# Staging buffers, store order, u quarters and store queues in the table stage, and the engine of two adds in the transform, of a two-part kernel

## The chip, the cores and the metric

The kernel runs on one core of a Trainium2 chip. The metric is the device time of one execution in microseconds (us). Before the change, three executions took 2489.95, 2495.92 and 2499.25 us; the median, 2495.92 us, is the time before. The profiled execution has a span of 2497.5 us, and the clock granted to TensorE was 0.968 of full speed on average over it.

Engines are named as the profile names them: PE is TensorE's matmul side and PEld its weight loads, DVE is VectorE, ACT is ScalarE, POOL is GpSimd, SP is SyncE, which here only issues transfers. A `q` behind an engine's name marks the transfers that the engine issues.

## The reference, cut to what matters

Two independent results are computed and laid side by side. Part A is attention with a recurrent memory: 64 segments of 32 rows, each with 8 rows of memory that come out of the segment before it, so that the 64 steps can't be reordered. Part B is a long convolution whose kernel is made from tables of exponentials and angles, done with Fourier transforms.

```python
def _A_ref(x, mem0, Wq, Wk, Wv, Wo, seg_len):          # x: 1 x 2048 x 1024, 32 heads of 128
    mem = mem0
    for s in range(n_seg):
        h = concatenate([mem, x[segment s]])
        q, k, v = h @ Wq, h @ Wk, h @ Wv
        o = softmax(mask(q k^T * scale)) v @ Wo
        mem = o[:, :M, :]; outs.append(o[:, M:, :])

def _B_ref(u, A_re, A_im, B_re, B_im, C_re, C_im, log_dt, Dskip):   # u: 1 x 2048 x 1024, N = 128
    dt = exp(log_dt); logdA = dt * (A_re + 1j * A_im); dB = dt * (B_re + 1j * B_im)
    P = exp(logdA[:, :, None] * l)                     # l = 0 .. 2047
    K = einsum('dn,dnl,dn->dl', C, P, dB).real         # the convolution kernel
    y = irfft(rfft(u, padded) * rfft(K, padded))[:2048]
    return y + u * Dskip

out = concatenate([_A_ref(...), _B_ref(...)], axis=-1)
```

## The kernel before: the parts that the change touches

The program has three stages on the one core. Up to about 500 us it makes part B's tables in 17 frames, and between the table instructions it runs three side jobs: the projections of part A that don't depend on the memory (`P` in the frame's order), the transform of u (`U`) and the turning of the transform's matrices (`M`). Up to about 746 us follows the transform of the convolution kernel with the pointwise products, then the last inverse transforms; from about 815 us on part A's 64 segments run, with the weights that don't fit on the chip loaded again in each segment.

Side job P, slice by slice. A value slice goes from PSUM into a staging tile `vst` and from there to DRAM; a key or query slice goes into one large tile `kst`, whose eight stores are put into a list, `late`, from which every later eviction takes one. `kst` is a single buffer: the next matrix's first eviction can write it only when all eight stores of the matrix before have landed.

```python
slices = [k0 0-7, v0 0-3, q0 0-7, v0 4-7, k1 0-7, v1 0-3, q1 0-7, v1 4-7]      # shortened
for i, (m, t, c) in enumerate(slices):
    for j in range(2):
        a = take([128, 512], F32, "pro")               # PSUM
        ...                                            # 8 or 16 matmuls
        def evict(copy, ...):                          # m == "v"
            if late:
                late.pop(0)()
            vst = vals.tile([128, 2, 2, 128], BF16, name="vst", tag="vst", bufs=3)
            copy(out=vst..., in_=a[:])
            nc.sync.dma_start(out=self.PVd[t]..., in_=vst...)
        def evict(copy, ...):                          # m == "k" or "q"
            if late:
                late.pop(0)()
            if (m, t) not in stage:
                stage[m, t] = self.pool.tile([128, NS, 4, 4, XL], BF16, name="kst", tag="kst")
            copy(out=stage[m, t][:, :, h, g, :], in_=a[:]...)
            # after the 16th: late gets 8 stores PKd<-kst
        if j == 0 and i + 3 < len(slices):
            ws.append(load(i + 3))                     # wsl, 4 buffers, on SyncE's queue
        yield evict
```

Side job U, the transform of u, in quarters `dq` of 256 channels:

```python
def load_uh(dh):                                       # half of the channels, one buffer
    t_ = up.tile([128, 16, DH], BF16, name="u_h", tag="u_h")
    for r in range(4):
        sy.dma_start(out=t_[:, 4 * r:4 * r + 4, :], in_=u_r[r][:, :, DH * dh:DH * dh + DH])
...
for dq in range(4):
    if dq % 2 == 0:
        uv = load_uh(dq // 2)
    for kc in range(4):
        for r in (0, 2, 1, 3):
            ...                                        # 8 matmuls ups<-u_h,MF, evictions, adds on DVE and POOL
```

The kernel values are stored to DRAM (`Kd`) in 30 small pieces for each of four groups; one piece leaves after each exponential, and what is left at the end leaves alternately on SyncE's and GpSimd's queue:

```python
def put(out, in_):
    late.append(lambda eng=gp: eng.dma_start(out=out, in_=in_))
...
for n_, f_ in enumerate(late):                         # at the end of the tables
    f_((sy, gp)[n_ % 2])
```

The pointwise stage: two halves `dh` of the channels, four row blocks `kc`, two `half`. With `dh == 1` two inverse transforms of the other half follow each.

```python
for half in range(2):
    ...                                                # 32 matmuls hps, copy of one result by ACT
    X = pw.tile(...)
    v.tensor_tensor(out=X[:, 0], in0=s_[0][:], in1=o_[:], op=ALU.add)        # L1150
    v.tensor_tensor(out=X[:, 1], in0=s_[0][:], in1=o_[:], op=ALU.subtract)   # L1151
    Y = pw.tile([128, 2, 2, DH], F32, name="y", tag="y", bufs=2)
    for n_, q in enumerate(qs):
        v.tensor_tensor(out=Y[:, n_]..., in0=uc, in1=x_, op=ALU.mult)        # L1157
        v.tensor_tensor(out=x_, in0=un, in1=x_, op=ALU.mult)                 # L1158
    v.tensor_tensor(out=Y[:, :, 0, :], ...)                                  # L1159
    v.tensor_tensor(out=Y[:, :, 1, :], ...)                                  # L1160
    for j, op in ((0, ALU.add), (1, ALU.subtract)):
        (v if (dh, kc, half) == (1, 3, 1) else gp).tensor_tensor(out=Bt[:, kc, half, j], ...)   # L1163
    inverses(2 if dh == 1 else 0)                      # ends with two DVE instructions on uu: L1215, L1216
...
if dh == 0 and kc == 0:
    ks.append(load_k(1, (sy,), ...))                   # 31 loads KT<-Kd for the second half
```

Of the kernel before, what the change touches and what calls it, by code (L numbers as in the profile page):

```python
# [10 lines left out]
BF16 = mybir.dt.bfloat16  # L11
F32 = mybir.dt.float32
# [52 lines left out]
class Ahead:  # L65
# [40 lines left out]
    def projections(self):  # L106

        nc, KC, NS, XL, PKd, xTl = self.nc, self.KC, self.NS, self.XL, self.PKd, self.xTl

        slices = [(m, t, c) for m, t, cs in (("k", 0, (0, 8)), ("v", 0, (0, 4)), ("q", 0, (0, 8)), ("v", 0, (4, 8)), ("k", 1, (0, 8)), ("v", 1, (0, 4)),  # L110
                                             ("q", 1, (0, 8)), ("v", 1, (4, 8))) for c in range(*cs)]

        def load(i):
            m, t, c = slices[i]
            w = self.pool.tile([128, KC, 256], BF16, name="wsl", tag="wsl", bufs=4)
            nc.sync.dma_start(out=w[:], in_=self.src(m)[:, :, 2048 * t + 256 * c:2048 * t + 256 * c + 256].rearrange("k p f -> p k f"))
            return w
        ws = [load(0), load(1), load(2)]
        take, vals = yield
        late = []  # L120

        def rows_out(t):
            for k in range(XL):
                late.append(lambda k=k, t=t: nc.sync.dma_start(out=PKd[:].rearrange("s (h k) f -> k s h f", k=XL)[k][:, :, 512 + 128 * t:640 + 128 * t],
                                  in_=self.PVd[t][:].rearrange("(s k) (h e) -> k s h e", k=XL, e=128)[k]))

        done = {}
        stage = {}
        self.late = late

        def counted(m, t, n, then):
            done[m, t] = done.get((m, t), 0) + 1
            if done[m, t] == n:
                then()

        for i, (m, t, c) in enumerate(slices):
            w = ws[i]
            g, h2 = c // 2, 2 * (c % 2)
            mo = 256 * t + (0 if m == "k" else 128)
            for j in range(2):  # L140
                a = take([128, 512], F32, "pro")
                if m == "v":
                    for b in (2 * j, 2 * j + 1):
                        for kc in range(KC):
                            nc.tensor.matmul(a[:, 256 * (b % 2):256 * (b % 2) + 256], lhsT=xTl[:, kc, 16 * b:16 * b + 16, :].rearrange("p s k -> p (s k)"),
                                             rhs=w[:, kc, :], start=(kc == 0), stop=(kc == KC - 1), skip_group_check=True)

                    def evict(copy, a=a, t=t, c=c, j=j):
                        if late:
                            late.pop(0)()  # L150
                        vst = vals.tile([128, 2, 2, 128], BF16, name="vst", tag="vst", bufs=3)
                        copy(out=vst[:].rearrange("p b h e -> p (b h e)"), in_=a[:])
                        nc.sync.dma_start(out=self.PVd[t][:].rearrange("(b p) f -> p b f", p=128)[:, 2 * j:2 * j + 2, 256 * c:256 * c + 256],
                                          in_=vst[:].rearrange("p b h e -> p b (h e)"))
                        counted("v", t, 16, lambda: rows_out(t))
                else:
                    for kc in range(KC):
                        nc.tensor.matmul(a[:], lhsT=w[:, kc, 128 * j:128 * j + 128], rhs=xTl[:, kc, :, :].rearrange("p s k -> p (s k)"),  # L158
                                         start=(kc == 0), stop=(kc == KC - 1))

                    def evict(copy, a=a, m=m, t=t, g=g, h=h2 + j, mo=mo):
                        if late:
                            late.pop(0)()
                        if (m, t) not in stage:
                            stage[m, t] = self.pool.tile([128, NS, 4, 4, XL], BF16, name="kst", tag="kst")
                        st = stage[m, t]
                        copy(out=st[:, :, h, g, :], in_=a[:].rearrange("p (s k) -> p s k", k=XL))

                        def out():
                            for r in range(8):  # L170
                                late.append(lambda r=r: nc.sync.dma_start(out=PKd[8 * r:8 * r + 8, :, mo:mo + 128].rearrange("s p f -> p s f"),
                                                                          in_=st[:, 8 * r:8 * r + 8].rearrange("p s a b c -> p s (a b c)")))
                        counted(m, t, 16, out)
                if j == 0 and i + 3 < len(slices):
                    ws.append(load(i + 3))
                yield evict
# [420 lines left out]
def part_b(ctx, tc, u, A_re, A_im, B_re, B_im, C_re, C_im, log_dt, Dskip, out_b, ahead, copies, residents):  # L597
# [5 lines left out]
    DH, DQ = 512, 256  # L603
# [207 lines left out]

    u_r = u.rearrange("(c p r) d -> r p c d", p=128, r=4)

    def load_uh(dh):
        t_ = up.tile([128, 16, DH], BF16, name="u_h", tag="u_h")
        for r in range(4):
            sy.dma_start(out=t_[:, 4 * r:4 * r + 4, :], in_=u_r[r][:, :, DH * dh:DH * dh + DH])
        return t_[:].rearrange("p c (t s e) -> p c s t e", t=4, e=8)


    def take(shape, dtype, name):
        return ps_k.tile(shape, dtype, name=name, tag="s")
# [13 lines left out]

    def side():

        for dq in range(4):
            if dq % 2 == 0:  # L840
                uv = load_uh(dq // 2)
            for kc in range(4):
                got = {}
                for r in (0, 2, 1, 3):
                    ps = take([128, 2, DQ], F32, "ups")
                    for cs in range(2):
                        for mc in range(4):
                            pe.matmul(ps[:, cs, :], lhsT=MF[:, 4 * r + mc, cs, 128 * kc:128 * kc + 128], rhs=uv[:, 4 * r + mc, 8 * (dq % 2):8 * (dq % 2) + 8],
                                      start=(mc == 0), stop=(mc == 3), skip_group_check=True)

                    def evict(copy, r=r, ps=ps, got=got, dq=dq, kc=kc):
                        if r == 0:
                            got["a"] = up.tile([128, 2, 2, DQ], F32, name="ua", tag="ua")
                        a_ = got["a"]
                        if r < 2:
                            copy(out=a_[:, r], in_=ps[:])
                            return
                        s_ = got[r] = up.tile([128, 2, 2, DQ], F32, name="us", tag="us", bufs=3)
                        v.tensor_tensor(out=s_[:, 0], in0=a_[:, r - 2], in1=ps[:], op=ALU.add)
                        v.tensor_tensor(out=s_[:, 1], in0=a_[:, r - 2], in1=ps[:], op=ALU.subtract)  # L860
                        if r == 3:
                            e_, o_ = got[2], s_
                            x_ = up.tile([128, 4, 2, DQ], F32, name="ux", tag="ux")
                            gp.tensor_tensor(out=x_[:, 0], in0=e_[:, 0], in1=o_[:, 0], op=ALU.add)
                            gp.tensor_tensor(out=x_[:, 2], in0=e_[:, 0], in1=o_[:, 0], op=ALU.subtract)
                            for q, cs, op in ((1, 0, ALU.subtract), (1, 1, ALU.add), (3, 0, ALU.add), (3, 1, ALU.subtract)):
                                gp.tensor_tensor(out=x_[:, q, cs], in0=e_[:, 1, cs], in1=o_[:, 1, 1 - cs], op=op)
                            gp.dma_start(out=Ud[kc, dq], in_=x_[:])
                    yield evict
# [34 lines left out]
    late = []  # L904

    def put(out, in_):
        late.append(lambda eng=gp: eng.dma_start(out=out, in_=in_))

    def put_values(sb):
        kx = KxT["t"]  # L910
# [215 lines left out]
    def pointwise(dh, kc, KT, Bt):  # L1126
        us = spectra.pop(0)
        for half in range(2):
# [20 lines left out]
            X = pw.tile([128, 2, 2, DH], F32, name="x", tag="x")  # L1149
            v.tensor_tensor(out=X[:, 0], in0=s_[0][:], in1=o_[:], op=ALU.add)  # L1150
            v.tensor_tensor(out=X[:, 1], in0=s_[0][:], in1=o_[:], op=ALU.subtract)  # L1151
            Y = pw.tile([128, 2, 2, DH], F32, name="y", tag="y", bufs=2)
            split = "p c (a d) -> p c a d"
            for n_, q in enumerate(qs):
                uc, un = (us[q][:, :, i, :].unsqueeze(1).to_broadcast([128, 2, 2, DQ]) for i in range(2))
# [4 lines left out]
            v.tensor_tensor(out=Y[:, :, 1, :], in0=Y[:, :, 1, :], in1=X[:, :, 0, :], op=ALU.add)  # L1160
            first = 0 if half == 0 else 1
            for j, op in ((0, ALU.add), (1, ALU.subtract)):
                (v if (dh, kc, half) == (1, 3, 1) else gp).tensor_tensor(out=Bt[:, kc, half, j], in0=Y[:, first], in1=Y[:, 1 - first], op=op)  # L1163
            inverses(2 if dh == 1 else 0)

    NIV = 3
# [55 lines left out]
    for dh in range(2):  # L1222
# [8 lines left out]
        for kc in range(4):  # L1231
            pointwise(dh, kc, ks[dh], Bt)
            if kc < 3 or dh == 0:
                spectra.append(load_u(dh + (kc + 1) // 4, (kc + 1) % 4))
            if dh == 0 and kc == 0:
                ks.append(load_k(1, (sy,), ktp.tile([128, 16, DH], BF16, name="KT", tag="KT")))
    ctx2.close()
    ctx_m.close()
    for c in range(16):
# [97 lines left out]
```

## Time and profile before

| Of the profile's page | value |
|---|---|
| span | 2497.5 us |
| PE busy | 2021.1 us, 81% |
| DVE busy | 1480.5 us, 59% |
| ACT busy | 965.7 us, 39% |
| POOL busy | 411.4 us, 16% |
| vst, 128x512, evicted by DVE | 20 times, mean 681 ns |
| vst, 128x512, evicted by ACT | 12 times, mean 582 ns |
| kst, 128x512, evicted by DVE / ACT | 43 times, mean 685 ns / 21 times, mean 581 ns |
| Bt on POOL, 128x1024 | 30 times, mean 2556 ns |
| Bt on DVE, 128x1024 | 2 times, mean 1222 ns |
| Kd stores issued by POOL / SP | 102 / 18 |

How to read it: busy times are sums over the span, and the three stages have different limits. A group's row gives the engine, the tile written and the tile read, the count and the mean of one. The row of an engine's waits names who released it last. A time line gives for each instruction its start, its length and, in brackets, how long the engine sat idle before it and who ended that.

### The profile page before, as it was taken

The page shows a single profiled execution, that of the slowest core. Times are in us where ns is not written, and L with a number is a line of the kernel's source. Part 1 is how long each engine was busy: PE and PEld are TensorE (multiplying, and loading weights), DVE is VectorE, ACT ScalarE, POOL GpSimd, SP SyncE. Part 2 cuts the span into 40 slices and gives each one's busy share as a digit, 9 for nine tenths or more (in the row PEclk, how much of TensorE's full clock was granted, in tenths as well). Part 3 has the DMA queues.
Part 4 walks back from the last instruction along what each step waited for, and adds up shares of the span by engine and source line. Part 5 has one row for each costly group of instructions (what it writes and reads, how often), then busy time and mean ns, then how long its engine had stood idle before and what let it go on. Part 6 is the DMA issues. An engine that isn't in the chain of part 4 may idle for free.

```text
span 2497.5 us, 76340 instructions
## 1 busy us (share of the span) xinstructions
PE 2021.1 (81%) x32774; PEld 1080.4 (43%) x32774; DVE 1480.5 (59%) x3129; ACT 965.7 (39%) x1543; POOL 411.4 (16%) x628
## 2 busy tenths in 40 slices
PE   1689888785968688888888888887888888888879
PEld 1356564532423244444444444444444444444444
DVE  9589888979791354545454545454545454545540
ACT  6679788811212132333333323232323233333321
POOL 2235565634331100000000000000000000000010
PEclk9999999888989799999999999999999999999999
DMA  6675965654339999999999999999999999999992
GB/s 161 191 217 167 272 167 149 167 162 144 107 132 347 346 378 378 374 390 365 380 378 373 363 369 387 370 367 359 383 377 371 385 378 380 379 384 374 389 368 90
DMA packets 384778, 763.17 MB, mean 306 GB/s; under 512 B 119462, under 2 KB 213638, under 8 KB 382390
## 3 DMA queue, kind: packets, MB, share of 16 engines
q1 hardware_dynamic: 365638, 702.56, 78.3%
q0 software_dynamic: 13888, 37.89, 4.6%
q10 hardware_dynamic: 4912, 17.84, 2.0%
q8 instruction: 256, 4.19, 0.7%
q14 instruction: 84, 0.69, 0.1%
HBM read 703.35 MB, written 67.88 MB: 309 GB/s over the span
## 4 chain that ended last, share of the span: by engine, by line
DMA 31%; PE 23%; DVE 8%; ACT 3%; issue 2%; SPq 1%; ACTq 0%; DVEq 0%
DMA wst<-WD_k 15%; PE acc L339 13%; DMA wst<-WD_o 11%; PE pp L438 3%; DMA wst<-WD_v 3%; PE pe L561 2%; PE tr L350 2%; DMA wst<-WD_q 1%; DVE piece L278 1%; ACT ev L345 1%; DMA W_o<-in_A_Wo_dram 1%; PE pv L411 1%; DVE ob L527 1%; ACT ob L528 1%; DVE sc L378 1%
## 5 line engine op out<-in xcount | busy, mean ns | idle before, releaser
L339 PEld LDWEIGHTS <-hT 128*32 128x32 bf16 x12352 | 326.0, 97 | 467.4 <-issue 245.4
L339 PE MATMUL acc<-wst,hT 128*32 128x512 bf16 x3072 | 312.6, 391 | 158.9 <-DMA wst<-WD_k 66.2
L345 ACT CAST ev<-acc 128x512 bf16<-128x512 f32 x384 | 225.1, 586 | 406.5 <-PE acc L339 401.6
L438 PEld LDWEIGHTS <-oT 128*32 128x32 bf16 x8192 | 203.1, 96 | 124.4 <-issue 97.8
L278 DVE TENSOR_SCALAR piece<-keep 128x256 int32<-128x256 int32 (+1 forms) x640 | 191.2, 363 | 52.4 <-PE pp L438 32.5
L438 PE MATMUL pp<-W_o,oT 128*32 128x256 bf16 x5120 | 210.6, 275 | 7.5 <-DMA W_o<-in_A_Wo_dram 7.5
L339 PE MATMUL acc<-W_v,hT 128*32 128x512 bf16 x3072 | 210.9, 379 | 0.0
L377 DVE TENSOR_REDUCE mx<-sc 128x8 f32<-128x320 f32 x128 | 62.4, 488 | 247.0 <-PE sc L370 246.7
L339 PE MATMUL acc<-W,hT 128*32 128x512 bf16 x2560 | 206.2, 393 | 0.0
L351 DVE COPY KT<-tr 128x512 bf16<-128x512 bf16 x64 | 27.2, 425 | 260.5 <-PE tr L350 260.5
L358 POOL COPY KT<-pk 128x128 bf16<-128x128 bf16 x128 | 37.7, 295 | 809.2 <-PE sc L370 444.5
L438 PE MATMUL pp<-wst,oT 128*32 128x256 bf16 x2560 | 128.7, 277 | 45.4 <-DMA wst<-WD_o 36.1
L351 ACT COPY QT<-tr 128x512 bf16<-128x512 bf16 x128 | 75.0, 586 | 190.5 <-PE tr L350 189.6
L1209 PE MATMUL yp<-Bt,mi 128*128 128x512 bf16 x384 | 112.3, 400 | 44.2 <-DMA mi<-MId 32.4
L312 POOL COPY hT<-xt 128x192 bf16<-128x192 bf16 x64 | 22.2, 348 | 729.3 <-DMA xt<-XTd 574.4
L425 ACT CAST oT<-pv 128x512 bf16<-128x512 f32 x128 | 75.0, 586 | 166.4 <-PE pv L411 165.0
L339 PE MATMUL acc<-W_q,hT 128*32 128x512 bf16 x1792 | 134.7, 382 | 0.0
L158 PE MATMUL pro<-xTl,wsl 128*128 128x512 bf16 x512 | 121.7, 389 | 5.2 <-ACT xTl L102 5.2
L379 ACT ACTIVATE sc<-sc 128x320 f32<-128x320 f32 x128 | 54.0, 422 | 154.2 <-DVE sc L378 148.8
L339 PE MATMUL acc<-W_k,hT 128*32 128x512 bf16 x1536 | 108.7, 390 | 0.0
L1137 PE MATMUL hps<-KT,MF 128*128 128x512 bf16 x384 | 96.4, 402 | 15.0 <-DVE x L1151 14.4
L350 PE MATMUL tr<-a_ident,ev 128*128 128x128 bf16 x1024 | 101.8, 222 | 1.0 <-ACT KT L351 1.0
(280 smaller groups left out, 3700.4 us busy)
## 6 DMA issues: line engine op xcount, KB each, us to landing
wst<-WD_o SPq DMA_DIRECT2D x320, 512.0 KB
wst<-WD_k SPq DMA_DIRECT2D x256, 512.0 KB
wst<-WD_q SPq DMA_DIRECT2D x256, 512.0 KB
wst<-WD_v SPq DMA_DIRECT2D x256, 512.0 KB
Ud<-ux POOLq DMA_DIRECT2D x16, 1024.0 KB, 5.7
uq<-Ud SPq DMA_DIRECT2D x32, 512.0 KB
pk<-PKd SPq DMA_DIRECT2D x64, 192.0 KB
wsl<-in_A_Wk_dram SPq DMA_DIRECT2D x16, 512.0 KB
```

Of the source, the lines that this page charges most:

```text
L158: nc.tensor.matmul(a[:], lhsT=w[:, kc, 128 * j:128 * j + 128], rhs=xTl[:, kc, :, :].rearrange("p s k -> p (s k)"), start=(kc == 0), stop=( ...
L278: nc.vector.tensor_scalar(out=out.bitcast(I32), in0=in_.bitcast(I32), scalar1=0, scalar2=None, op0=ALU.bitwise_or)
L339: nc.tensor.matmul(a[32 * g:32 * g + 32, o_:o_ + rhs.shape[1]], lhsT=hT[:, kc, :], rhs=rhs, start=(kc == 0), stop=(kc == KC - 1), tile_pos ...
L345: nc.scalar.copy(out=q[:], in_=a[:])
L350: nc.tensor.transpose(out=p[:, i, hl, :, :].rearrange("p a b -> p (a b)"), in_=q[:, 128 * hl:128 * hl + 128], identity=ident[:])
L351: eng(out=dst, in_=p[:, i, :, :, :])
L377: nc.vector.tensor_reduce(out=mx[:], in_=sc, axis=AX.X, op=ALU.max)
L379: nc.scalar.activation(out=sc, in_=sc, func=ACT.Exp, scale=scale)
L425: nc.scalar.copy(out=o[:], in_=p[:].rearrange("p a (g q) -> p a g q", g=4))
L438: nc.tensor.matmul(po[32 * qt:32 * qt + 32, :], lhsT=oT[:, h % 4, (h % 16) // 4, :], rhs=columns(w, 1024 * hh + 256 * qt, 256)[0][1], star ...
L1137: pe.matmul(ps[:, cs, :], lhsT=MF[:, 4 * rr + mc, cs, 128 * kc:128 * kc + 128], rhs=rhs, start=(i == 0 and mc == 0), stop=(i == 1 and mc = ...
L1209: pe.matmul(yp[:], lhsT=m_[:, cs, kc, :], rhs=Bt[:, kc, half, j, c_, :], start=(n == 0), stop=(n == 15))
```

## The change

It touches two stages. In the table stage it gives the value staging tile six buffers, takes up to two stores from the list at every eviction, loads u by quarters of the channels into two tiles (so that the next quarter can be loaded while one is used), and puts the kernel-value stores on SyncE's queue. In the transform it puts the two last pointwise instructions on VectorE throughout, with one buffer for Y, and moves the second half's kernel loads to GpSimd's queue. The aim of the first part is to take away waits for buffers in the tables. The diff, with unchanged lines cut:

```diff
                     def evict(copy, a=a, t=t, c=c, j=j):
-                        if late:
+                        for _ in range(min(2, len(late))):
                             late.pop(0)()
-                        vst = vals.tile([128, 2, 2, 128], BF16, name="vst", tag="vst", bufs=3)
+                        vst = vals.tile([128, 2, 2, 128], BF16, name="vst", tag="vst", bufs=6)
...
                     def evict(copy, a=a, m=m, t=t, g=g, h=h2 + j, mo=mo):
-                        if late:
+                        for _ in range(min(2, len(late))):
                             late.pop(0)()
...
-    def load_uh(dh):
-        t_ = up.tile([128, 16, DH], BF16, name="u_h", tag="u_h")
-        for r in range(4):
-            sy.dma_start(out=t_[:, 4 * r:4 * r + 4, :], in_=u_r[r][:, :, DH * dh:DH * dh + DH])
+    u_q = u.rearrange("(c p r) (d t q s) -> r d q p c t s", p=128, r=4, d=2, t=4, q=2)
+    def load_uq(dq):
+        t_ = up.tile([128, 16, 4, 64], BF16, name="u_h", tag="u_h%d" % (dq % 2))
+        for c in range(16):
+            sy.dma_start(out=t_[:, c], in_=u_q[c // 4][dq // 2][dq % 2][:, c % 4])
...
+        uvs = [load_uq(0), load_uq(1)]
         for dq in range(4):
-            if dq % 2 == 0:
-                uv = load_uh(dq // 2)
+            uv = uvs.pop(0)
+            if dq in (1, 2):
+                uvs.append(load_uq(dq + 1))
...
-        late.append(lambda eng=gp: eng.dma_start(out=out, in_=in_))
+        late.append(lambda eng=sy: eng.dma_start(out=out, in_=in_))
...
-            Y = pw.tile([128, 2, 2, DH], F32, name="y", tag="y", bufs=2)
+            Y = pw.tile([128, 2, 2, DH], F32, name="y", tag="y")
...
-                (v if (dh, kc, half) == (1, 3, 1) else gp).tensor_tensor(out=Bt[:, kc, half, j], in0=Y[:, first], in1=Y[:, 1 - first], op=op)
+                v.tensor_tensor(out=Bt[:, kc, half, j], in0=Y[:, first], in1=Y[:, 1 - first], op=op)
...
-                ks.append(load_k(1, (sy,), ktp.tile([128, 16, DH], BF16, name="KT", tag="KT")))
+                ks.append(load_k(1, (gp,), ktp.tile([128, 16, DH], BF16, name="KT", tag="KT")))
```

More of the change, by code (lines that the diff above doesn't have):

```diff
@@ L812, in part_b @@
     u_r = u.rearrange("(c p r) d -> r p c d", p=128, r=4)
-    def load_uh(dh):
-        t_ = up.tile([128, 16, DH], BF16, name="u_h", tag="u_h")
-        for r in range(4):
-            sy.dma_start(out=t_[:, 4 * r:4 * r + 4, :], in_=u_r[r][:, :, DH * dh:DH * dh + DH])
-        return t_[:].rearrange("p c (t s e) -> p c s t e", t=4, e=8)
+    u_q = u.rearrange("(c p r) (d t q s) -> r d q p c t s", p=128, r=4, d=2, t=4, q=2)
[3 more added lines that the diff above has]
+            sy.dma_start(out=t_[:, c], in_=u_q[c // 4][dq // 2][dq % 2][:, c % 4])
+        return t_[:].rearrange("p c t (s e) -> p c s t e", e=8)
     def take(shape, dtype, name):
@@ L847, in side @@
                         for mc in range(4):
-                            pe.matmul(ps[:, cs, :], lhsT=MF[:, 4 * r + mc, cs, 128 * kc:128 * kc + 128], rhs=uv[:, 4 * r + mc, 8 * (dq % 2):8 * (dq % 2) + 8],
+                            pe.matmul(ps[:, cs, :], lhsT=MF[:, 4 * r + mc, cs, 128 * kc:128 * kc + 128], rhs=uv[:, 4 * r + mc],
                                       start=(mc == 0), stop=(mc == 3), skip_group_check=True)
```

## The prediction, made before the changed kernel ran

> **What bounds the kernel now.** I read the chain of waits first, to see which stage a change can move, then the time lines of the two stages that the change touches, and the table of waits of the table stage.
>
> ```profile
> ## 4 chain that ended last, share of the span: by engine, by line
> DMA 31%; PE 23%; DVE 8%; ACT 3%; issue 2%; SPq 1%; ACTq 0%; DVEq 0%
> ```
>
> The chain, followed backwards, reaches only to 819.88 us, where part A's segments start. From there it is weight transfers (DMA 31%) and matmuls, which the change leaves alone. So part A keeps its length, and the change counts by how far it moves the end of the pointwise stage (746 us): after that the DMA engines are 88 to 104% busy with weights that need the memory freed there, so I carry a shift of that point over one to one.
>
> The table stage, read from ScalarE's time line. Each frame loads the exponential table once, so the distance of two such loads is a frame:
>
> ```profile
> 201.97 1.28 ACT L1003 ACT_TABLE_LOAD   x1
> 224.99 1.28 ACT L1003 ACT_TABLE_LOAD   x1
> 248.00 1.28 ACT L1003 ACT_TABLE_LOAD   x1
> 273.49 1.28 ACT L1003 ACT_TABLE_LOAD   x1
> 303.66 1.28 ACT L1003 ACT_TABLE_LOAD   x1
> ```
>
> Two frames take 23.02 us, the next ones 25.49 and 30.17. In the 23 us frames ACT is busy 94% and DVE 95%, which is their floor. The waits of 70 to 520 us say what the longer frames wait for:
>
> ```profile
> ACT vst L152 <- DMA PVd<-vst: 12.2, 4, 4.5
> DVE kst L167 <- DMA PVd<-vst: 8.7, 2, 4.6
> ACT kst L167 <- DMA PVd<-vst: 4.5, 2, 2.6
> ACT kst L167 <- DMA PKd<-kst: 2.2, 1, 2.2
> PEld L848 <- DMA u_h<-in_B_u_dram: 1.0, 1, 1.0
> ```
>
> (Total us, times, longest.) The first row is the three staging tiles used up. The next three are one thing: the first eviction of a new matrix waits for the single kst buffer; that two rows name PVd I take as the view's choice of the transfer that came last. The u load is nearly free of waits.
>
> The pointwise stage, from the time lines of DVE and POOL:
>
> ```profile
> 526.27 4.66 POOL L1163 TENSOR_TENSOR Bt<-y 128x1024 bf16<-128x1024 f32 x2 [8.72 <-DMA Dsk<-in_B_Dskip_dram]
> 529.13 1.23 DVE L1150 TENSOR_TENSOR x<-hps,osb__7233 128x1024 f32<-128x1024 f32 x1 [3.09 <-ACT osb__7233 L1145]
> ...
> 538.77 1.23 DVE L1150 TENSOR_TENSOR x<-hps,osb__7322 128x1024 f32<-128x1024 f32 x1
> ...
> 542.29 3.25 DVE L1158 TENSOR_TENSOR x<-uq,x 128x1024 f32<-128x1024 f32 x1
> ...
> 638.35 0.42 DVE L1215 TENSOR_TENSOR uu<-uu,Dsk 128x512 bf16<-128x512 bf16 x1
> 638.52 4.95 POOL L1163 TENSOR_TENSOR Bt<-y 128x1024 bf16<-128x1024 f32 x2 [10.55 <-DVE y L1160]
> 638.88 2.38 DVE L1216 TENSOR_TENSOR uu<-uu,yb 128x512 bf16<-128x512 bf16 x1
> 641.18 2.57 DVE L1215 TENSOR_TENSOR uu<-uu,Dsk 128x512 bf16<-128x512 bf16 x1
> 643.86 0.43 DVE L1216 TENSOR_TENSOR uu<-uu,yb 128x512 bf16<-128x512 bf16 x1
> ```
>
> The reader is to see that DVE runs without gaps here (it is the bound of this stage), and that an instruction that takes 0.42 or 1.23 us takes about 2 us more while POOL's Bt instruction runs.
>
> **What the Trainium skill says.** "SBUF — State Buffer", section "Who interferes with whom": a VectorE instruction with two SBUF inputs contends with a GpSimd instruction that reads SBUF; who comes first holds the shared ports for the whole instruction. The lines above agree: 2.38 against 0.43 us. The same section infers that writing descriptors for a transfer issued by GpSimd does not disturb two-input instructions; no line here shows it, and I need it for the 31 kernel loads that move to POOL. "DMA: Bandwidth & Descriptors", section "Why small descriptors are slow (HBM only)", gives a fixed cost per packet. The trace's DMA records agree: packets of 256 bytes on SyncE's queue took 18 ns, of 512 bytes 27, of 1024 bytes 46. "TensorE: Matmul & The Clock Gate", section "What's actually happening", says that idleness throttles TensorE. The trace agrees: where the kst wait is (280 to 290 us) the clock fell to 0.66.
>
> **The change part by part.**
>
> Tables. The distances from 123.44 us on are 23.03, 26.68, 28.82, 23.02, 23.01, 25.49, 30.17, 23.03, 23.01, 26.78, 29.58, 23.01, 23.02, 23.51. Over 23.02 they add to 3.66 + 2.47 + 3.76 + 0.49 = 10.4 us in the frames of the vst wait and 5.80 + 7.15 + 6.56 = 19.5 us in those of the kst wait. The latter hold about 4 us of wait and after it matmuls at half clock. Six vst buffers cover the six value evictions of one frame (144.0 to about 161 us; the seventh comes at 171 us), so the 10.4 go. With two stores per eviction the eight kst stores leave in four evictions, about 156 instead of 172 us, and the next matrix starts at about 177 us; stores land within 10 us, so the 19.5 go too. Of 29.9 us I take 27, with 3 for new waits on SyncE's queue.
>
> That queue gets 84 kernel-value stores and 64 u loads in place of 8. In the built program every transfer on it waits for the one eight places ahead. At 0.5 to 0.8 us each, as in this trace (18 such stores took 14.03 us), a frame's some 25 transfers need about 17 of 23 us: full, but not the bound. The u quarters are runs of 128 bytes. From 32-byte packets at 15 ns and 256-byte ones at 18 I estimate 16 ns: 8192 packets x 16 ns / 16 engines = 8.2 us per quarter. The first two quarters, 32 issues x 0.55 us = 17.6 us, push the next weight slice from 95.87 to about 111 us; PE needs it at about 120 us. No gain and no loss; the u wait removed is about 1 us.
>
> The seam of the stages. The built program has nine more kernel-value stores on SyncE's queue between the 31 first kernel loads and the last stores; 9 x 0.6 = 5 us. The last stores, which before were issued up to 522.7 us and released POOL's first Bt at 526.27, come 5 us later against the rest. That wait moves to DVE, because Bt lies where the kernel values did: DVE would reach its first Bt at 516.5 + 8 x 1.2 = 526.2, and waits until about 531. Loss 5 us.
>
> Pointwise, first half. A period now: (597.54 - 538.77) / 5 = 11.75 us, of which 9.64 (529.13 to 538.77) is undisturbed work. New: 9.64 + 2 x 1.15 for Bt = 11.95. The first two periods were undisturbed already and so get 2.3 us longer; of the first, 1.6 fits into a gap of 3.09. Sum to the start of the last period: +3.3 us. The second half begins with the mi loads, which wait for DVE's last reading of uq, and that comes 2.3 us earlier in a period without POOL: together +1.0, with the seam +6.
>
> Pointwise, second half. There POOL delays two uu instructions by 2 us each, 4.1 us per period. In place of it come 2.3 us of Bt plus some 0.1. So 15.30 becomes 13.9 (PE needs 64 matmuls x 0.217 = 13.9, which is the new floor), 21.03 becomes 19.4, and 19.24 becomes 17.6. Three of the first and three of the others: 3 x 1.4 + 3 x 1.6 = 9 us. I take 7, since waits for uq (5.64, 3.87 and 3.85 us) and mi hang on transfers and can give some back.
>
> Sum: -27 + 5 + 1 - 7 = -28 us. 2495.9 - 28 = 2468 us.
>
> **The rivals.** First: SyncE's queue becomes the bound of the tables. For it: in-order issue, eight in flight, 140 transfers more, and stretches with the DMA engines over 100% busy (150 to 160 us). Then value and weight transfers come late, frames stay at 25 to 30 us, and the change is worth 0 to -10 us. Against it: the queue stood idle for some 15 us in every frame without value slices. Second: moving Bt to DVE costs its full price, 30 x 1.22 = 37 us, with the contention of now hidden in waits anyway; then transform +15 to +20 and the sum is about -5. Against it: DVE has no gaps in the first half, so the delays by POOL are real time. Third: the seam costs nothing and the second half gives its 9 us; sum -36. Fourth: part A's start is set by DMA work that goes on anyway, so that a part of the gain is lost there; little speaks for it, since those loads wait for the memory of the stage before.
>
> **Range and chances.** The before itself spreads over 9 us. The table gain is safe to perhaps 8 us, seam and transform to about 6 each: 2452 to 2484 us holds it 8 times in 10. 2% is 50 us, more than all the parts together can give (29.9 + 9), so faster by over 2% gets 0.05; slower by over 2% would need the first two rivals and more, 0.02; within 2% 0.93.
>
> **What would show each step.** Frames all near 23.0 us between the table loads, no wait of vst or kst for a store, and PE's clock near 1.0 from 280 to 290 and 380 to 390 us: the table step. The end of the tables (last KxT eviction, 506.1 us) near 479 us. A DVE wait of about 5 us before its first Bt: the seam. Bt on DVE 32 times at 1.22 us, L1158 and L1216 never above 1.3 and 0.5 us, periods of 12 us in the first half and 14 to 19 in the second: the transform. Wrong I would be by frames above 24 us whose waits name wsl, u_h or Kd, by PE waits in the pointwise stage beyond those for mi, or by a first segment of part A that does not move with 746 us.

## The result and the profile after

The changed kernel takes 2458.59 us (median of 4 executions, 2452.7 to 2462.8) against 2497.59 us before: a ratio of 0.9843, 95% interval 0.9805 to 0.9881. Predicted were 2468 us, with a range of 2452 to 2484 us, and a gain below 2%; the gain is 39.0 us where 28 were predicted. The table lays the two profiles side by side at the points at which the prediction's steps end.

| point in the trace | before, us | after, us | moved | prediction |
|---|---|---|---|---|
| last KxT eviction (end of the tables) | 506.11 | 476.83 | -29.3 | -27 |
| second X (past the seam) | 529.13 | 499.59 | -29.5 | -22 |
| second X of the second half | 628.90 | 599.51 | -29.4 | -21 |
| last Bt (end of the pointwise stage) | 746.23 | 706.44 | -39.8 | -28 |
| weight load wst<-WD_k at the start of part A's segments | 819.88 | 781.65 | -38.2 | -28 |
| end of the span | 2497.5 | 2459.8 | -37.7 | -28 |

The chain of waits on the page of the changed kernel:

```profile
## 4 chain that ended last, share of the span: by engine, by line
DMA 33%; PE 30%; DVE 15%; issue 13%; ACT 6%; SPq 1%; POOL 1%; DVEq 0%; ACTq 0%; POOLq 0%
```

Its shares add up to 99% where those of before added up to 68%: it is followed back to the start of the span now. But between 516 and 753 us most of it is "issue", time in which the view names no wait; the longest piece, 79.6 us from 515.94 us on, is the time before GpSimd's first store of a result. So the chain doesn't show what bounds the pointwise stage, and VectorE's time line is used for that below. DMA and PE still carry most of the chain. The last three rows of the table show that the shift of the pointwise stage's end reaches the end of the program almost whole.

The frames, from ScalarE's time line of the changed kernel (start, length, engine, line; line numbers are 3 higher than before):

```profile
238.96 1.28 ACT L1006 ACT_TABLE_LOAD   x1
261.98 1.28 ACT L1006 ACT_TABLE_LOAD   x1
285.00 1.28 ACT L1006 ACT_TABLE_LOAD   x1
```

All distances are 23.0 us; only one of the fourteen behind the first frame is longer than 23.04 (23.41 us). The excess over the floor fell from 29.9 to 0.4 us. The waits of 70 to 520 us, cut to the rows in which a write to a staging tile waits:

```profile
DVE kst L167 <- PE pro L158: 17.4, 4, 7.6
...
ACT kst L167 <- PE pro L158: 7.7, 3, 3.7
```

What is left are waits for matmuls (PE pro), that is for the tile's input; these stood in the kernel before too (20.3 and 7.2 us). All rows that name a store are gone. TensorE's granted clock from 280 to 290 us, 0.66 before, is 1.00.

The pointwise stage, from VectorE's time line of the changed kernel:

```profile
496.60 2.36 DVE L1166 TENSOR_TENSOR Bt<-y 128x1024 bf16<-128x1024 f32 x2
...
620.15 1.23 DVE L1160 TENSOR_TENSOR y<-uq,x 128x1024 f32<-128x1024 f32 x1 [4.54 <-DMA uq<-Ud]
```

The first Bt has no bracket: VectorE doesn't wait for it, and the seam costs nothing. The groups of instructions by shape give the trade on VectorE, first of the kernel before, then of the changed one (busy us, mean ns of one | idle before):

```profile
L1158 DVE TENSOR_TENSOR x<-uq,x 128x1024 f32<-128x1024 f32 x32 | 47.3, 1478 | 1.1
...
L1215 DVE TENSOR_TENSOR uu<-uu,Dsk 128x512 bf16<-128x512 bf16 x32 | 28.5, 891 | 13.8 <-DMA uu<-in_B_u_dram 13.6
```

```profile
L1161 DVE TENSOR_TENSOR x<-uq,x 128x1024 f32<-128x1024 f32 x32 | 39.2, 1225 | 1.1
...
L1166 DVE TENSOR_TENSOR Bt<-y 128x1024 bf16<-128x1024 f32 x32 | 37.8, 1222 | 0.5
...
L1218 DVE TENSOR_TENSOR uu<-uu,Dsk 128x512 bf16<-128x512 bf16 x32 | 13.5, 420 | 13.0 <-DMA uu<-in_B_u_dram 13.0
```

L1158 (now L1161) falls by 8.1 and L1215 (now L1218) by 15.0 us. Of the groups not shown, L1157 falls from 45.5 to 39.0 and L1216 from 27.3 to 13.6 us; that is 43.3 us in all. Bt adds 37.8 us less the 2.4 of its two instructions of before, 35.4 us. VectorE ends with 8 us less work than before in these groups, although it got 30 instructions more. The waits for uq (one of them is the last line of the time line above) stay as they were, 13.4 us before and 13.1 after.

How far a total can be trusted: in one set, 54 executions of the kernel before lay between 2477.96 and 2511.51 us. In the profiles of this study the part behind the pointwise stage, which is the same program throughout, took 1737 to 1753 us. Below, stage ends therefore carry the reasons (those of the changed kernel agreed within 2 us in two profiles: 706.44 and 708.21), and totals are given with their intervals.

### The profile page after: what moved, and what is told of

Same layout as the page of the kernel before. It is cut to its first block, busy times and chain, and to the rows that moved or that the text cites. A ratio compares the mean times of both kernels' runs of the same rounds, so it can differ in the third digit from the quotient of the medians.

```text
span 2459.8 us, 76393 instructions
## 1 busy us (share of the span) xinstructions
PE 2017.1 (82%) x32774; PEld 1082.4 (44%) x32774; DVE 1470.8 (60%) x3159; ACT 963.6 (39%) x1543; POOL 303.5 (12%) x545
## 4 chain that ended last, share of the span: by engine, by line
DMA 33%; PE 30%; DVE 15%; issue 13%; ACT 6%; SPq 1%; POOL 1%; DVEq 0%; ACTq 0%; POOLq 0%
DMA wst<-WD_k 15%; PE acc L339 13%; DMA wst<-WD_o 10%; PE pp L438 3%; DMA wst<-WD_q 3%; PE pe L561 2%; PE pro L158 2%; DMA wst<-WD_v 2%; DVE nr L1029 2%; PE tr L350 2%; PE ups L851 2%; PE pa L998 1%; DVE piece L278 1%; ACT ev L345 1%; ACT E L1006 1%
## 5 line engine op out<-in xcount | busy, mean ns | idle before, releaser
L438 PE MATMUL pp<-wst,oT 128*32 128x256 bf16 x2560 | 129.0, 278 | 39.4 <-DMA wst<-WD_o 30.1
```

Source lines behind the costliest of these rows:

```text
L438: nc.tensor.matmul(po[32 * qt:32 * qt + 32, :], lhsT=oT[:, h % 4, (h % 16) // 4, :], rhs=columns(w, 1024 * hh + 256 * qt, 256)[0][1], star ...
```

## The experiments

### The table edits alone (e1_tables)

On the kernel before, in both evictions and at the value tile:

```diff
-                        if late:
+                        for _ in range(min(2, len(late))):
...
-                        vst = vals.tile([128, 2, 2, 128], BF16, name="vst", tag="vst", bufs=3)
+                        vst = vals.tile([128, 2, 2, 128], BF16, name="vst", tag="vst", bufs=6)
```

> The kernel before with only the two edits of the table evictions: six staging tiles for values and two stores per eviction. Kernel value stores stay on GpSimd, u stays in halves, Bt stays on GpSimd. Theory (the 29.5 us of the tables come from the two staging waits alone): all frames from 123 us on take 23.0 us, the last KxT eviction comes near 477 us instead of 506, the pointwise stage keeps its length, and the time is about 29 us less, 2468. Rival (the other queue and the u quarters had a part in it): some frames stay at 24 to 28 us, and 5 to 15 us of the gain are missing, 2475 to 2485.

Measured: 2484.31 us, ratio 0.9962 (0.9943 to 0.9982). The last KxT eviction comes at 494.49 us, 11.6 earlier and not 29. All frames take 23.0 us (one 23.37) but one, which ScalarE's time line shows between these two loads:

```profile
286.11 1.28 ACT L1003 ACT_TABLE_LOAD   x1
326.15 1.28 ACT L1003 ACT_TABLE_LOAD   x1
```

40.04 us in place of 23.0, and TensorE's time line says why:

```profile
298.98 1.89 PE L848 MATMUL ups<-u_h,MF 128*128 128x256 bf16 x8 [16.59 <-DMA u_h<-in_B_u_dram]
```

TensorE stands 16.59 us for the second half of u, for which the profile of before showed a wait of 1.0 us. So the rival holds, and by more than it said: the staging edits without the u quarters give less than half of the tables' gain.

### Each of the two edits alone (e5_vst and e6_two)

```diff
-                        vst = vals.tile([128, 2, 2, 128], BF16, name="vst", tag="vst", bufs=3)
+                        vst = vals.tile([128, 2, 2, 128], BF16, name="vst", tag="vst", bufs=6)
```

> The kernel before with six value staging tiles as the only edit. Theory (two separate waits, the rows that name the value stores for the kernel staging tile are the view's choice): the ScalarE wait of vst is gone, and the frames that begin with a new projection matrix keep 5 to 7 us over 23.0; excess of the frames about 20 us in place of 29.9, plus whatever of the u wait shows once the frames before it are faster. Rival (one cause: value stores hold up the kernel staging tile too): excess under 5 us apart from a u wait.

```diff
-                        if late:
+                        for _ in range(min(2, len(late))):
```

> The kernel before with two stores per eviction as the only edit. Theory: the kst waits are gone, the vst waits stay or grow; excess of the frames about 10 us in place of 29.9, plus whatever of the u wait shows. Rival (the staging tile of the kernels is free only after value stores land, so that earlier issue does not help): excess 25 us or more.

Measured with six tiles alone: excess 19.6 us, as the theory said, nearly all of it in three frames of 29.57, 29.86 and 28.73 us (both kernels of this section ran once, so only their frames and waits are read); two of the waits (total, times, longest) that are left:

```profile
DVE kst L167 <- DMA PVd<-vst: 10.3, 2, 5.3
...
PE ups L848 <- DMA u_h<-in_B_u_dram: 1.6, 1, 1.6
```

Value tiles are plentiful here, and the row of the kernel tile still names PVd: reading them as the view's choice of the last transfer was right. With two stores alone:

```profile
PE ups L848 <- DMA u_h<-in_B_u_dram: 15.4, 1, 15.4
ACT vst L152 <- DMA PVd<-vst: 15.1, 4, 5.4
```

No kst row that names a store is left, but the excess is 32.7 us, more than before, and the last KxT eviction comes at 509.67 us. That is a total in the range of the rival, but without its cause: the kst waits are gone, as the theory said. The vst waits grew from 12.2 to 15.1 us, and the u wait came out. Taken with e1, this orders the three waits: the u wait is 1.6 us where the kst waits stand, and 15 to 17 us in both kernels where they are gone. They hide it.

### The u halves in the changed kernel (e8_uh)

```diff
-    def load_uq(dq):
-        t_ = up.tile([128, 16, 4, 64], BF16, name="u_h", tag="u_h%d" % (dq % 2))
-        for c in range(16):
-            sy.dma_start(out=t_[:, c], in_=u_q[c // 4][dq // 2][dq % 2][:, c % 4])
+    def load_uh(dh):
+        t_ = up.tile([128, 16, DH], BF16, name="u_h", tag="u_h")
+        for r in range(4):
+            sy.dma_start(out=t_[:, 4 * r:4 * r + 4, :], in_=u_r[r][:, :, DH * dh:DH * dh + DH])
```

> The changed kernel with u in two halves of four issues again, one tile. Theory (the 17 us wait for u seen when only the table edits were made comes from the single u tile, filled only after its last reader, behind other transfers on SyncE's queue): one frame at 277 to 310 us takes about 40 us, all others 23.0; last KxT eviction near 494 instead of 477 us; about 2474. Rival (the wait came from kernel value stores on GpSimd, and is gone with them on SyncE): no such frame, 2459.

Measured: 2475.5 us, ratio 0.9918 (0.99 to 0.9937). One frame takes 40.14 us, all others 23.02 to 23.05, and the last KxT eviction comes at 494.33 us: in the changed kernel the u quarters are worth 17.5 us. The kernel value stores are on SyncE here; e1, with them on GpSimd, has the same wait, so the rival, GpSimd's stores as the cause, is out. SyncE's own time line of this kernel, and TensorE's next line, show the wait's parts:

```profile
288.18 0.58 SPq L116 DMA_DIRECT2D wsl<-in_A_Wk_dram  x1
288.87 6.47 SPq L817 DMA_DIRECT2D u_h<-in_B_u_dram  x4
```

```profile
297.86 1.89 PE L848 MATMUL ups<-u_h,MF 128*128 128x256 bf16 x8 [15.91 <-DMA u_h<-in_B_u_dram]
```

TensorE has been idle since 297.86 - 15.91 = 281.95 us, so from then on the tile has no reader and could be loaded. The load is issued only at 288.87, because the queue works through other transfers first (PKd, Kd, WD_o and, as the first line shows, a weight slice): 6.9 us. The other 9.0 us pass from the issue of the load to its landing. The clock follows: from 280 to 300 us it is 0.65 here and 1.00 in the changed kernel. This agrees with the Trainium skill, "TensorE: Matmul & The Clock Gate", section "What's actually happening", that idleness throttles TensorE.

### The queue edits alone (e3_queues)

On the kernel before: the u quarters as in the change, and

```diff
-        late.append(lambda eng=gp: eng.dma_start(out=out, in_=in_))
+        late.append(lambda eng=sy: eng.dma_start(out=out, in_=in_))
```

> The kernel before with only the two queue edits: kernel value stores of the frames on SyncE instead of GpSimd, u loaded by quarters with 64 issues. Theory (neither is on the path; they only make room): frames with value slices keep their excess of about 30 us in all, time 2495 to 2500. Rival (SyncE's queue becomes a bound while the staging tiles are still few, since each value store now stands behind kernel value stores): frames get longer, 2505 to 2515.

Measured: 2494.14 us, ratio 1.0012 (0.9984 to 1.0039); excess of the frames 31.0 us, last KxT eviction 508.23. The theory holds: without the staging edits these two edits gain nothing that can be measured, and SyncE's queue does not become a bound. So the parts don't add: staging edits alone 11.6 us, the two queue edits alone nothing, all together 29 us.

### Kernel value stores back on GpSimd (e7_kd_gp)

On the changed kernel, the edit of e3's diff the other way round.

> The changed kernel with the kernel value stores of the frames on GpSimd's queue again; u quarters, six value tiles and two stores per eviction stay. Theory (the move of these stores to SyncE has no part in the gain, and GpSimd's descriptor writing does not slow VectorE): all frames 23.0 us, last KxT eviction within 2 us of 477, pointwise as in the changed kernel, 2459. Rival (GpSimd falls behind, and VectorE waits for the KxT tile): frames of 24 us and more, 2465 to 2475.

Measured: 2457.04 us, ratio 0.9852 (0.9825 to 0.988); the changed kernel in the same set 0.9858 (0.9833 to 0.9883). In the total no part of the move can be seen. In the profile the last KxT eviction comes at 482.87 us, 5.9 later than in the changed kernel's profile of that set (477.01), which neither theory said: the first table load came 1.2 later, the first frame was 1.5 longer, and one frame took 26.29 us, in which TensorE waited 3.0 us for a weight slice.

The wait for a weight slice also stood in one frame of the next experiment (27.67 us), where these stores are on SyncE, cost 0.4 us in the first profile of the changed kernel and no frame is lengthened in its second. It can't be put down to the moved stores; where the other 2.7 us come from stays open. What the wait hangs on is seen on SyncE's time line of the changed kernel:

```profile
288.39 14.22 SPq L819 DMA_DIRECT2D u_h<-in_B_u_dram  x16
302.72 0.45 SPq L116 DMA_DIRECT2D wsl<-in_A_Wk_dram  x1
```

The 16 issues of the last u quarter stand directly ahead of the slice. In the four profiles (changed kernel twice, this one, the next) the slice is issued at 302.72, 301.51, 305.81 and 305.06 us, and TensorE's wait for it ends 4.3 to 4.5 us later in each; the wait is 1.8, 1.2, 3.0 and 4.4 us. So it depends on when the slice is issued. How late that is differs from run to run: the 16 issues took 13.0 to 18.2 us, and in the next experiment the queue was 3.6 us behind when it came to them.

### All left-over stores on SyncE (e4_seam)

```diff
-        f_((sy, gp)[n_ % 2])
+        f_(sy)
```

> The changed kernel with all 36 stores left over at the end of the tables on SyncE instead of half of them on GpSimd. Theory (in the changed kernel the stores land shortly before VectorE needs the memory, so that a delay within the slack is free and beyond it costs one to one): issues at 0.77 us end near 507 instead of 493 us, VectorE waits 10 to 13 us before its first Bt, and the uq loads behind them can add some; 2470 to 2478. Rival (the seam has large slack and never shows): no such wait, 2459.

Measured: 2463.66 us, ratio 0.9889 (0.9861 to 0.9917). SyncE issues the 36 stores until 508.90 us, and VectorE's time line shows the wait that the changed kernel lacks:

```profile
510.09 2.36 DVE L1166 TENSOR_TENSOR Bt<-y 128x1024 bf16<-128x1024 f32 x2 [8.20 <-DMA Kd<-KxT]
```

The theory holds, with 8.2 us for 10 to 13. VectorE was released 1.2 us after the last issue. In the changed kernel the last issue on SyncE ended at 493.19 us; with the same 1.2 us its memory was free near 494.4 us (an estimate), and VectorE came at 496.60: a slack of some 2.2 us. The pointwise stage ends at 720.02 us, 13.6 later than in the changed kernel: 4.6 from the end of the tables (the slice wait above), 0.8 before the first X (the changed kernel's second profile has 1.0 there), 8.2 from the wait. Only the 8.2 us are the edit's. Nothing of them is hidden later in the stage. The total is below the expected range, and 3 to 5 us above the medians of the changed kernel, 2458.59 and 2460.43 us; with an interval of 7 us to either side it can neither show nor contradict the 8.2 us. The part behind the stage took 1737 us here, the shortest of the study.

### The pointwise edits alone (e2_transform)

On the kernel before:

```diff
-            Y = pw.tile([128, 2, 2, DH], F32, name="y", tag="y", bufs=2)
+            Y = pw.tile([128, 2, 2, DH], F32, name="y", tag="y")
...
-                (v if (dh, kc, half) == (1, 3, 1) else gp).tensor_tensor(out=Bt[:, kc, half, j], in0=Y[:, first], in1=Y[:, 1 - first], op=op)
+                v.tensor_tensor(out=Bt[:, kc, half, j], in0=Y[:, first], in1=Y[:, 1 - first], op=op)
...
-                ks.append(load_k(1, (sy,), ktp.tile([128, 16, DH], BF16, name="KT", tag="KT")))
+                ks.append(load_k(1, (gp,), ktp.tile([128, 16, DH], BF16, name="KT", tag="KT")))
```

> The kernel before with only the pointwise edits: all of Bt on VectorE, one y buffer, the second 31 kernel loads on GpSimd's queue. Theory (VectorE only pays back the delays that GpSimd caused it in the first half, and wins in the second): tables as before, first half of the pointwise stage within 3 us, second half 10 us shorter, 2487. Rival (Bt costs its full price, 30 x 1.15 us): 2520 or more; between them, if other waits take up a part: 2497.

Measured: 2485.68 us, ratio 0.9976 (0.9956 to 0.9996). The tables end where they did (506.18 us). From the first X to the second X of the second half 114.91 us (before 112.40), from there to the last Bt 107.22 us (before 117.33): +2.5 - 10.1, and the stage ends 7.5 us earlier. The rival, Bt at its full price, is out. The groups of instructions show the same trade as in the changed kernel, without any edit of the tables:

```profile
L1158 DVE TENSOR_TENSOR x<-uq,x 128x1024 f32<-128x1024 f32 x32 | 39.2, 1225 | 1.1
```

In e3, which has the other edits of queue and u but leaves Bt on GpSimd, this group takes 47.3 us as before. So the time that VectorE gets back comes with the pointwise edits. Which part the single y buffer and the kernel loads' queue have in it was not separated.

The +2.5 are what Bt costs in the first half; the changed kernel has them too (+2.6 to the start of the last period of that half) and makes them good in the period before the second X of the second half, which takes 17.02 us there and 19.41 here (19.53 before). Why it stays long here is open.

### A version that goes further (e9_ahead, e10_after, e11_ahead)

What VectorE still waits for in the second half of the pointwise stage, behind the second X, are three loads of uq. SyncE's time line of the changed kernel shows the four uq loads behind a load of uu, whose tile must first be stored:

```profile
614.71 0.33 SPq L1177 DMA_DIRECT2D uu<-in_B_u_dram  x1
615.09 2.81 SPq L966 DMA_DIRECT2D uq<-Ud  x4
```

Ahead of the first of them the queue had stood since 605.6 us, with the uq loads behind it. The edit issues two of them as soon as VectorE has read their predecessors, in the same bytes:

```diff
-    def load_u(dh, kc):
+    def load_u(dh, kc, qs=(0, 2, 1, 3)):
...
-        for q in (0, 2, 1, 3):
+        for q in qs:
...
+            if dh == 1 and kc < 3:
+                more = load_u(1, kc + 1, ((0, 2), (1, 3))[half])
+                if half == 0:
+                    spectra.append(more)
+                else:
+                    spectra[-1].update(more)
             inverses(2 if dh == 1 else 0)
...
-            if kc < 3 or dh == 0:
+            if dh == 0:
```

> The changed kernel, with the loads of the next uq tiles in the second half of the pointwise stage issued in two parts: two tiles as soon as VectorE has read their predecessors in the first half period, two in the second, ahead of the inverse loads on SyncE's queue. The bytes are the same. Theory (VectorE's three waits of 4.0 to 4.5 us for uq come from the queue order): they are gone, the periods of 17.7 to 18.2 us come down to about 13.7, the pointwise stage ends 12 us earlier, about 2447. Rival (the queue then delays the inverse matrices instead, and TensorE waits for mi): 0 to -4 us.

> The changed kernel as it is, on the same chip as the two others of this set, so that they can be compared. Both theories: last KxT eviction near 477, pointwise stage to about 707 us, ratio to the kernel before about 0.984.

> The version with the uq loads issued in two parts, once more and beside the changed kernel. Theory: 11 us below the changed kernel, as its stage ends (695 against 706 us) say, ratio about 0.980. Rival (the weight transfers after 706 us give it back): no difference from the changed kernel.

Measured: 2450.1 us, ratio 0.9833 (0.9801 to 0.9865) in the first set; in the second, beside the changed kernel at 2460.43 us and 0.9858 (0.9833 to 0.9883), 2444.47 us and 0.9798 (0.9774 to 0.9823). VectorE's time line of the second:

```profile
615.14 1.23 DVE L1153 TENSOR_TENSOR x<-hps,osb__7926 128x1024 f32<-128x1024 f32 x1
629.02 1.23 DVE L1153 TENSOR_TENSOR x<-hps,osb__8034 128x1024 f32<-128x1024 f32 x1 [0.22 <-ACT osb__8034 L1148]
```

Periods of 13.88 us, as here, and 13.75 us in turn, in place of 13.57 to 13.75 and 17.7 to 18.4; the waits for uq are gone, and before this instruction 0.22 us of waiting are left, for TensorE's results by way of ACT. The stage ends at 696.21 us, 12.0 before the changed kernel's 708.21. The medians differ by 16 us, with intervals of some 6 us to either side of each. The theory holds, and this is the fastest version.

## Why the prediction was right, and where it was not

**Where the time is read.** The reading that part A keeps its length and takes over a shift of the pointwise stage's end one to one held: -39.8 us there, -38.2 at the first segment, -37.7 at the end. That the two ends agree within 2 us is luck in part, since the part behind the stage spreads over 16 us from profile to profile. That it starts earlier because memory is freed earlier, as the prediction says, was not tested by itself.

**The sum of the tables.** -27 predicted, -29.3 measured; the 3 us kept back for new waits were not needed. The excess over the frames' floor was the right measure, since it contains every wait, seen or hidden.

**Its parts.** Here the working failed, in the term "the u wait removed is about 1 us". The two staging edits, which were to bring all of it, bring 11.6 us by themselves (e1), and the u quarters 17.5 us on top of the rest (e8). The 1.0 us in the table of waits was what the kst waits had left of it. The split of the excess into 10.4 us for vst and 19.5 us for kst was right as an account of the kernel before (six tiles alone leave 19.6 us), but not as a list of what each edit gives: two stores alone give nothing. That the sum came out is luck to this extent: the change happened to contain the u quarters. Without them the tables would have gained some 12 us and not 27.

**SyncE's queue.** "Full, but not the bound" held: e3 loses no measurable time, and frames are at 23.0 us in the changed kernel. The first two u quarters pushed the weight slice from 95.87 to 112.08 us, about as predicted (111), and the frame there got no longer (30.1 us, 30.2 before). The push that cost time was the last quarter's, 0 to 4.6 us by run, which the prediction did not name. The packets of 128 bytes took 12.7 ns on average where 16 were estimated. The move of the kernel value stores shows no effect in the total (e7).

**The seam.** +5 us predicted, none measured; this term failed, in two of its steps. First, the kernel stores (nine, by the prediction) that lie between the kernel loads and the last stores were counted as a delay. SyncE's time line of before and of after, from the kernel loads on:

```profile
468.91 21.17 SPq L936 DMA_DIRECT2D KT<-Kd  x31
490.19 1.79 SPq L153 DMA_DIRECT2D PVd<-vst  x2
493.63 11.54 SPq L124 DMA_DIRECT2D PKd<-PVd  x8
...
508.63 14.03 SPq L907 DMA_DIRECT2D Kd<-KxT  x18
```

```profile
437.74 20.91 SPq L939 DMA_DIRECT2D KT<-Kd  x31
...
460.59 4.17 SPq L910 DMA_DIRECT2D Kd<-KxT  x7
464.81 10.64 SPq L124 DMA_DIRECT2D PKd<-PVd  x8
...
479.42 13.77 SPq L910 DMA_DIRECT2D Kd<-KxT  x18
```

Eight kernel stores in 4.5 us are new (the seven shown and one of 0.33 us ahead of them). But before, the queue stood idle for 1.65 us ahead of the PKd loads; the kernel loads now start 39.1 us ahead of the last KxT eviction and not 37.2; and kernel and PKd loads took 0.3 and 0.9 us less. That is 4.8 us, and the last 18 stores start 2.6 us behind the last KxT eviction, where before it was 2.5. Second, the 526.27 us at which POOL's first Bt began was taken for the arrival of the stores. It was the arrival of Y: VectorE's last instruction on it ended at 524.82 + 1.22 = 526.04 us. So even a delay would have met a slack of some 2 us, as e4 then measured. The wait that the prediction described exists; it takes 8.2 us if one makes the queue 11 us longer.

**Pointwise, first half.** To the start of its last period +2.6 us (83.63 against 81.04), predicted +3.3; to the second X of the second half +0.1 (112.49 against 112.40), predicted +1. The prediction's own terms (0.7 and 2.3 us in the first two periods, 0.2 in each of five more) add up to 4.0 and not to 3.3. The first period cost nothing: its gap of 3.09 us shrank to 0.63 and took in all of Bt, not 1.6 us of it. The second cost 2.2 us, as predicted, and the five others 0.1 each.

**Pointwise, second half.** The working gave 9 us, 7 were taken, 10.4 measured (106.93 against 117.33). The short periods came to 13.6 to 13.7 us (13.9 predicted), the long ones to 17.7 to 18.2 (17.6 and 19.4). The deduction for uq and mi was one error; the waits for uq kept their 13 us and gave nothing back. The other was the floor of 13.9 us that TensorE was to set: the prediction's own 15.30 - 4.1 + 2.4 gives 13.6, which is what came. The floor did not show here, where only every second period is short; in e11, where all of them are, they take 13.7 to 13.9 us. The first long period also came down by more than said, from 21.03 to 18.21 us, 1.1 of it because its wait for uq fell from 5.64 to 4.54.

**The rivals.** The third, no cost at the seam and all of the second half's gain, is what came, with a sum of -36 (its terms -27, +1 and -9 make -35) against -37.7 in the span. The first, SyncE's queue as the bound, is out by the frames of 23.0 us, the second, Bt at its full price, by e2. For the fourth these two profiles leave 2 us, which is within their spread.

So of the 9 us by which the time came out below 2468, the tables have 2, the seam 5, the first half 1 and the second half 3, less 2 lost behind the stage, where profiles differ by more than that anyway.

## What to carry to other kernels

Take the gain of removing waits from the distance of a frame to its floor, not from the table of waits: a wait that another one covers shows 1 us there and costs 17 when the other goes, so several edits may be needed together, and one of them alone can look worthless (two stores per eviction, by themselves, gave nothing). Before taking the arrival of a transfer from the start of the instruction behind it, look whether another operand came last. Where one queue feeds a stage and a transfer that waits holds up those behind it, as SyncE's did here, look at the place of a load on it as well as at its size: splitting four loads into two pairs and issuing one pair some 10 us and the other over 25 us earlier brought 12 us without a byte less.

## What the runs showed of the hardware

GpSimd issued 31 kernel loads from 495.2 to 515.9 us, at some 0.53 us each, while VectorE ran instructions with two SBUF inputs on 128x1024 fp32: those took 1.22 to 1.23 us (L1160 and L1161), as elsewhere. The Trainium skill, "SBUF — State Buffer", section "Who interferes with whom", marks as inferred that such an instruction takes only the read side of the shared ports and that writing descriptors needs the write side; that the two don't disturb each other is measured here for the VectorE instruction. A GpSimd add on 128x1024, 2.56 us, cost VectorE some 43.3 / 30 = 1.4 us each on average (e2, with the pointwise edits alone, gives the same group times as the changed kernel to 0.1 us); done by VectorE it costs 1.2 us. So such an instruction was not free on the idle engine, although its own 2.56 us lay beside other work.
